# Top-32 attention feeding an expert layer: the eight fillers written by GpSimd in one operation, the weights' high halves rounded on ScalarE, and the order laid out anew

## The chip, the cores and the metric

The kernel runs on one core of a Trainium2 chip. The metric is the device time of one execution in microseconds (us). Engines are called as the profile calls them: PE is TensorE (PEld its weight loads), DVE is VectorE, ACT is ScalarE, POOL is GpSimd, SP is the queue that issues the DMAs.

## The reference, cut to what matters

```python
scores = scale * np.matmul(q, k.transpose(0, 1, 3, 2))      # 8 batches x 8 heads, 576 x 576, depth 64
kth = np.partition(scores, -32, axis=-1)[..., -32:-31]       # the 32nd largest of a row
mask = scores >= kth
scores = np.where(mask, scores, -1000000000.0)
attn = np.exp(scores - np.max(scores, axis=-1, keepdims=True))
attn = attn / (np.sum(attn, axis=-1, keepdims=True) + 1e-09)
x = np.matmul(attn, v)                                       # laid out as 4608 tokens x 512
...
r = np.maximum(x @ w_in, 0.0)                                # 512 -> 2048
out = (s * (r * r) + b) @ w_out                              # 2048 -> 512
```

The two weights arrive as 64-bit floats and are converted on the chip.

## The kernel before

**Tiles.** Attention runs over 288 tiles of 128 score rows by 576 columns. The expert layer runs over 18 blocks of 256 tokens, each in 16 chunks of 128 hidden units, so there are 288 chunks too. Products are taken with the operands split into a rounded high half and a remainder ("high" and "low"), which is why most operands exist twice (`ka`/`kb`, `ph`/`pl`, `gh`/`gl`, `wih`/`wil`, `woh`/`wol`). Batch 0 is kept whole, without low halves of the attention weights.

**One attention tile.** PE makes the scores in PSUM (L364), ACT copies them to `sc` (L370). DVE takes the eight largest of each of eight groups (L376) and works through the candidates with three more maxima and two replacements (L383 to L392); the last of them gives `wl`, whose column 15 is a cautious estimate of the 32nd largest. POOL makes a threshold from the high 16 bits of that estimate (`half`, L399) and the bias for the exponential (`max`, L404). ACT writes a sign for each score, minus above the threshold and plus below, and sums the signs into `cnt` (`side`, L411). POOL multiplies scores and signs into `wt` (`win`, L417). Behind the 576 signed scores stand 8 filler columns: some of them large and the rest very negative, so many of each, by the count, that the eighth largest of all 584 columns is just the 32nd largest score. DVE finds it (`wmax`, L435, into `chk`), then masks the exponentials that ACT made (`exp`, L429; `mask`, L439). PE transposes the masked tile into `tp` and `tq` (`put`, L468, L469), ACT and DVE split it (`high` L474, `low` L479), and PE multiplies with the values (L503 to L505).

**The fillers before.** They take three operations on two engines. `max` on POOL also zeroes the low 16 bits of `wl`'s column 15 (L405). `pad` on ACT writes eight signs from the count into a tile `pad` (L422), with two column operands (scale and bias). `fill` on ACT multiplies them with column 15 into the last eight columns of `wt` (L425), with one column operand; it waits for `win` and for `max`.

**The weights.** 64 pieces of 128 by 256 go through the chip: a load, three bit operations on DVE (`bits0` to `bits2`, L307 to L313), two squarings on ACT (`far0`, `far1`, L320 and L324) and a matmul (`far2`, L327) that guard the range, `whigh` on POOL (L330) that rounds the high half, and `wlow` on POOL (L333) that subtracts it. The pieces lie between the first tiles' work. The bank of PSUM in which `far2` adds up is the one that the hidden product `h` uses, so the expert layer starts when the last piece is through.

**One chunk of the expert layer.** PE makes `h` with 12 matmuls (L610), ACT applies relu and squares (L616, L619), POOL splits (`ghigh` L623, `glow` L627), PE adds 6 matmuls to the output (L633). At the end of a block DVE scales two results (L640) and SP stores them.

**What sets the order.** Every operation is entered into a list with its engine, a slot, a duration and an offset from the table `PARTS`. `Graph.order` plays the list through and gives each engine its fixed order; a tile's key is its number plus the offset, a chunk's key is `TURN0 + chunk / TURNS` plus the offset, a weight's key runs from 0 to `WTURN`. Among what could start within `SLACK` of the earliest, the smallest key goes first. Operations in `LOCK` (all of POOL's, DVE's `mask` and the bit operations) are kept from running on DVE and POOL at once in that play. On the chip each engine then runs its own order, and waits where an operand or a buffer isn't ready. There is one buffer each for `wt` and `sg`, two for `e`, four for `sc`.

## Time and profile before

| what | value |
|---|---|
| median of 3 runs | 1702.57 us (1700.66 to 1703.59) |
| the profiled execution | 1707.27 us, span 1705.5 us |
| before the expert layer starts | 0 to 305.6 us |
| attention and expert layer together | 305.6 to 1558 us |
| expert layer alone | 1558 to 1694 us |
| last store and the end | 1694 to 1705.5 us |

The span is the time from the first to the last instruction in the trace; the rest of the execution's time lies around it. The borders are read from the timeline: the first hidden matmul starts at 305.62 us, the last masked tile's work on DVE ends at about 1558 us, the last matmul of the expert layer ends at about 1694 us. A row of a group of instructions gives busy time, the mean duration in ns, the idle time of the engine just before, and what ended it. In a row of a tile the three durations are the least, the median and the largest. A row of waits gives the total in us, how many there were and the longest.

### The profile page before, as it was taken

To read this page: it belongs to the slowest core of one execution; us is meant where nothing else is said; L and a number is where in the kernel's file an instruction comes from. 1 tells how busy PE (TensorE), PEld (TensorE's weight loads), DVE (VectorE), ACT (ScalarE), POOL (GpSimd) and SP (SyncE) were. 2 spreads that over 40 slices of the span, in tenths; PEclk is the share of its full clock that TensorE was granted. 3 is DMA by queue.
4 is the path that set the end of the run, shared out by engine and by line. 5 is a ranking of instruction groups with operands and counts; after the bars stand their busy time and mean duration, and the time that the engine had idled before them with its cause. 6 is when DMAs were issued, how large, how long until landed. Compare 5 with 4: busy or idle time off the path is not lost. (4 is left out here: it accounts for less than half of the span.)

```text
span 1705.5 us, 34540 instructions
## 1 busy us (share of the span) xinstructions
PE 1494.9 (88%) x9361; PEld 1286.2 (75%) x9361; DVE 1404.7 (82%) x6055; ACT 1362.5 (80%) x3354; POOL 1233.6 (72%) x2176
## 2 busy tenths in 40 slices
...
GB/s 137 88 88 107 107 90 106 49 58 80 59 62 57 70 70 68 58 82 58 82 54 86 57 70 61 60 71 60 69 68 65 65 110 88 138 109 63 26 13 15
DMA packets 102123, 124.51 MB, mean 73 GB/s; under 512 B 30240, under 2 KB 65056, under 8 KB 101920
## 3 DMA queue, kind: packets, MB, share of 16 engines
...
q14 instruction: 126, 1.03, 0.2%
...
## 5 line engine op out<-in xcount | busy, mean ns | idle before, releaser
L417 POOL TENSOR_TENSOR wt<-sc,sg 128x576 f32<-128x576 f32 x288 | 399.7, 1388 | 95.7 <-ACT sg L411 40.3
L610 PE MATMUL h<-x,wih 128*128 128x256 f32 x2176 | 421.5, 288 | 17.4 <-ACT rt L616 16.4
L376 DVE MAX8 cand<-sc 128x8 f32<-128x72 f32 x2304 | 397.4, 219 | 34.6 <-ACT sc L370 32.1
L610 PEld LDWEIGHTS h<-x,wih 128*128 128x128 f32 x2176 | 347.6, 190 | 42.3 <-ACT rt L616 28.1
L610 PE MATMUL h<-x,wil 128*128 128x256 f32 x1088 | 307.3, 282 | 0.0
L439 DVE SCALAR_TENSOR_TENSOR e<-sc,chk,e 128x576 f32<-128x576 f32 x288 | 289.2, 1006 | 0.8
L435 DVE MAX8 chk<-wt 128x8 f32<-128x584 f32 x288 | 219.3, 761 | 50.2 <-ACT wt L425 40.9
L468 PE MATMUL tp<-idr,e 128*128 128x128 f32 x1152 | 191.2, 291 | 67.3 <-DVE e L439 38.0
L411 ACT ACTIVATE sg<-sc,nb 128x576 bf16<-128x576 int16 x288 | 221.7, 770 | 21.5 <-POOL nb L399 15.9
L370 ACT ACTIVATE sc<-s_ps 128x576 f32<-128x576 f32 x288 | 186.3, 647 | 64.8 <-DVE e L439 39.0
L627 POOL TENSOR_TENSOR gl<-rt,gh 128x256 fp32r<-128x256 f32 x288 | 220.8, 768 | 14.4 <-PE ops L633 3.8
L429 ACT ACTIVATE e<-sc,nb 128x576 f32<-128x576 f32 x288 | 221.9, 771 | 2.7 <-PE tq L469 2.5
L468 PEld LDWEIGHTS tp<-idr,e 128*128 128x128 f32 x1152 | 136.1, 147 | 115.0 <-DVE pl L479 38.8
L623 POOL TENSOR_SCALAR gh<-rt 128x256 fp32r<-128x256 f32 x288 | 127.5, 444 | 115.3 <-ACT rt L619 71.9
L610 PEld LDWEIGHTS h<-x,wil 128*128 128x128 f32 x1088 | 207.0, 190 | 0.0
L633 PE MATMUL ops<-woh,gh 128*128 128x512 f32 x576 | 192.8, 404 | 6.6 <-DVE osb L640 4.3
L474 ACT ACTIVATE ph<-tp 128x512 fp32r<-128x512 f32 (+1 forms) x288 | 171.1, 594 | 29.3 <-PE tp L468 26.2
L479 DVE TENSOR_TENSOR pl<-tp,ph 128x512 fp32r<-128x512 f32 x252 | 171.7, 681 | 26.5 <-ACT ph L474 23.5
L364 PE MATMUL s_ps<-ka,qs 128*128 128x288 f32 x512 | 164.5, 334 | 32.8 <-ACT sc L370 15.1
L633 PE MATMUL ops<-woh,gl 128*128 128x512 f32 x576 | 190.2, 402 | 0.4 <-POOL gl L627 0.4
L616 ACT ACTIVATE rt<-h 128x256 f32<-128x256 f32 x288 | 108.5, 377 | 101.7 <-PE h L610 96.5
L633 PE MATMUL ops<-wol,gh 128*128 128x512 f32 x576 | 188.0, 398 | 0.0
(101 smaller groups left out, 3502.1 us busy)
## 6 DMA issues: line engine op xcount, KB each, us to landing
...
qs<-ka SPq DMA_DIRECT2D x128, 64.0 KB, 2.0
qs<-kb SPq DMA_DIRECT2D x128, 64.0 KB, 2.0
```

The lines of the kernel that those rows point to most:

```text
L370: nc.scalar.activation(t.sc, t.flat, AF.Identity)
L376: nc.vector.max(t.cand[:, g * 8 : g * 8 + 8], t.sc[:, g * GW : (g + 1) * GW])
L411: nc.scalar.activation(t.sg, t.sc.bitcast(I16)[:, 1::2], AF.Sign, bias=t.half, scale=-1.0, accum_out=t.cnt[:, 0:1])
L417: nc.gpsimd.tensor_tensor(out=t.wt[:, :S], in0=t.sc, in1=t.sg, op=ALU.mult)
L429: nc.scalar.activation(t.e, t.sc, AF.Exp, bias=t.nb, scale=scale)
L435: nc.vector.max(t.pair.chk[:, t.i, 0:PADS], t.wt)
L439: nc.vector.scalar_tensor_tensor(t.e, t.sc, chk[:, PADS - 1 : PADS], t.e, op0=ALU.is_ge, op1=ALU.mult, accum_out=chk[:, PADS : PADS + 1])
L468: nc.tensor.transpose(tp[:, c, :], t.e[:, c * P : (c + 1) * P], idf)
L479: nc.vector.tensor_tensor(out=pl[:, :, dst], in0=t.tp, in1=ph[:, :, dst].bitcast(F32), op=ALU.subtract)
L610: nc.tensor.matmul(k.h, wi[a][:, cc, fs], k.x[cc][:, c, :], start=(cc == 0 and i == 0), stop=(cc == NCC - 1 and i == 2))
L627: nc.gpsimd.tensor_tensor(out=k.gl[fc], in0=k.rt[fc], in1=k.gh[fc].bitcast(F32), op=ALU.subtract)
L633: nc.tensor.matmul(k.ops[t], g[fc][:, t * P : (t + 1) * P], wo[w][:, fc, :], start=(fc == 0 and i == 0), stop=(fc == NFC - 1 and i == 2),)
```

## The change

The fillers become one operation on POOL, `pad`, ahead of `wmax`: it adds the count (a column) to a constant row and multiplies by -1e30, straight into the last eight columns of `wt`. The two operations on ACT, the memset in `max`, the tile `pad` and the column `one` go. `pad` needs `side` and `win`; `wmax` needs `pad`. The rounding of the weights' high halves goes from POOL to ACT, as an identity. The reduction of `chk` in `finish1` takes in one more column. The table's offsets, `SLACK` of POOL, `TURN0` and `WTURN` have other values, so each engine's order is another. The matmuls, the DMAs and the buffers other than `pad` are the same in number and size.

```diff
-    "whigh": ("POOL", 380, 430, 9.29), "wlow": ("POOL", 702, 740, -10.27), ...
+    "whigh": ("ACT", 306, 408, 9.29), "wlow": ("POOL", 702, 740, -6.52), ...
...
-    "half": ("POOL", 147, 190, -0.55), "max": ("POOL", 185, 230, -7.81), ...
+    "half": ("POOL", 147, 190, -0.68), "max": ("POOL", 125, 190, -7.26), ...
...
-    ... "pad": ("ACT", 70, 190, 1.55), "fill": ("ACT", 70, 190, -0.32), ...
+    ... "pad": ("POOL", 270, 310, -1.7), ...
...
-SLACK = {"PE": 0, "DVE": 86, "ACT": 0, "POOL": 67, "SP": 0}
-TURN0, TURNS = 48.1, 0.992
-WTURN = 34.2
+SLACK = {"PE": 0, "DVE": 86, "ACT": 0, "POOL": 0, "SP": 0}
+TURN0, TURNS = 49.4, 0.992
+WTURN = 40
...
-        nc.gpsimd.memset(pads[:, j : j + 1], -1.0 / (S - 2 * (TOPK - PADS + j) - 1))
-    one = const.tile([P, 1], F32, name="one")
-    nc.gpsimd.memset(one, 1.0)
+        nc.gpsimd.memset(pads[:, j : j + 1], float(2 * j - (S - 2 * (TOPK - PADS) - 1)))
...
         def high(w):
-            nc.gpsimd.tensor_scalar(w.dst[0][:, w.a, w.cs], w.lw.bitcast(F32), 1.0, 0.0, op0=ALU.mult, op1=ALU.add)
+            nc.scalar.activation(w.dst[0][:, w.a, w.cs], w.lw.bitcast(F32), AF.Identity)
...
         nc.gpsimd.tensor_scalar(t.nb, t.wl[:, 0:1], -scale, 0.0, op0=ALU.mult, op1=ALU.add)
-        nc.gpsimd.memset(t.wl.bitcast(I16)[:, 30:31], 0)
...
     def pad(t):
 
-        t.pad = sb.tile([P, PADS], F32, name="pad", tag="pad", bufs=BUFS["pad"])
-        nc.scalar.activation(t.pad, pads, AF.Sign, scale=t.cnt[:, 0:1], bias=one)
-
-    def fill(t):
-        nc.scalar.activation(t.wt[:, S:], t.pad, AF.Identity, scale=t.wl[:, 15:16])
+        nc.gpsimd.tensor_scalar(t.wt[:, S:], pads, t.cnt[:, 0:1], -PADK, op0=ALU.add, op1=ALU.mult)
...
-        nc.vector.tensor_reduce(tmin[:, 0, pr.i : pr.i + 1], pr.chk[:, :n, PADS - 1], axis=AX.X, op=ALU.min)
+        nc.vector.tensor_reduce(tmin[:, 0, pr.i : pr.i + 1], pr.chk[:, :n, PADS - 1 :], axis=AX.XY, op=ALU.min)
...
-            pb = Buf("pad")
-            pd = part("pad", i, lambda t=t: pad(t), [side_], [pb], [cnt])
-            pd = part("fill", i, lambda t=t: fill(t), [pd, win, mx], use=[pb, wt, wl])
+            pd = part("pad", i, lambda t=t: pad(t), [side_, win], use=[wt, cnt])
```

What the new order moves is shown at three places. The line numbers of the changed kernel are a few lower than those of the kernel before for the same operation.

The first is PE where the expert layer starts: `tp` and `tq` are a tile's transposes, `h` with `gh` the last pieces of the weights' guard, `h` with `x` the first hidden product. Before:

```order
L505 MATMUL av<-p_2974,vst 128x320
L327 MATMUL h<-gh,idr 128x256
L468 MATMUL tp<-idr,e 128x128 x4
L469 MATMUL tq<-idr,e 64x128
L610 MATMUL h<-x,wih 128x256 x2
L610 MATMUL h<-x,wil 128x256
L610 MATMUL h<-x,wih 128x256 x2
L610 MATMUL h<-x,wil 128x256
L364 MATMUL s_ps<-ka,qs 128x288
```

The same place in the changed kernel:

```order
L315 MATMUL ops<-x,bmat 128x256
L462 MATMUL tp<-idr,e 128x128 x4
L463 MATMUL tq<-idr,e 64x128
L326 MATMUL h<-gh,idr 128x256
L363 MATMUL s_ps<-ka,qs 128x288
L363 MATMUL s_ps<-kb,qs 128x288
L363 MATMUL s_ps<-ka,qs 128x288
L363 MATMUL s_ps<-kb,qs 128x288
L604 MATMUL h<-x,wih 128x256 x2
L604 MATMUL h<-x,wil 128x256
```

Counted from the start of PE's order, 44 tiles' transposes stand ahead of the first hidden matmul before, and 50 in the changed kernel. Ahead of the last tile's transposes stand 244.75 of the 288 chunks' hidden matmuls before, and 247 in the changed kernel.

The second is POOL in the stage in which both layers run: `wt` from `sc` and `sg` is `win`, `nb` from `wl` are `half` and `max`, `gh` and `gl` belong to the expert layer, `avu` is the sum of two halves of a result. Before:

```order
L417 TENSOR_TENSOR wt<-sc,sg 128x576
L623 TENSOR_SCALAR gh<-rt 128x256
L627 TENSOR_TENSOR gl<-rt,gh 128x256
L417 TENSOR_TENSOR wt<-sc,sg 128x576
L399 TENSOR_SCALAR nb<-wl 128x1
L404 TENSOR_SCALAR nb<-wl 128x1
L405 MEMSET wl 128x1
L530 TENSOR_TENSOR avu<-avu,avl 128x576
```

The changed kernel, with `wt` from `pads` and `cnt` the new `pad`:

```order
L415 TENSOR_TENSOR wt<-sc,sg 128x576
L398 TENSOR_SCALAR nb<-wl 128x1
L419 TENSOR_SCALAR wt<-pads,cnt 128x8
L403 TENSOR_SCALAR nb<-wl 128x1
L699 TENSOR_TENSOR kb<-kr,ka 128x576
L617 TENSOR_SCALAR gh<-rt 128x256
L415 TENSOR_TENSOR wt<-sc,sg 128x576
L621 TENSOR_TENSOR gl<-rt,gh 128x256
L419 TENSOR_SCALAR wt<-pads,cnt 128x8
```

The memset is gone and `pad` stands behind `win`, here with a `half` and then with a `gl` between them. Over all 288 tiles `pad` follows `win` at once in 73; a `half` or a `max` of another tile stands between them in 97, and a longer operation (a split, a sum, a spread) in most of the others.

The third is ACT in the stage with the weights: `x` from `x` is `far0`, `gh` is `far1`, `sg` is `side`. Before:

```order
L411 ACTIVATE sg,cnt<-sc,nb 128x576
L422 ACTIVATE pad<-pads,one,cnt 128x8
L513 ACTIVATE avu<-av 64x320
L320 ACTIVATE x<-x 128x256
L324 ACTIVATE gh<-x,mid 128x256
L320 ACTIVATE x<-x 128x256
L324 ACTIVATE gh<-x,mid 128x256
L370 ACTIVATE sc<-s_ps 128x576
```

The changed kernel:

```order
L409 ACTIVATE sg,cnt<-sc,nb 128x576
L507 ACTIVATE avu<-av 64x320
L319 ACTIVATE x<-x 128x256
L329 ACTIVATE wih<-x 128x256
L323 ACTIVATE gh<-x,mid 128x256
L409 ACTIVATE sg,cnt<-sc,nb 128x576
L369 ACTIVATE sc<-s_ps 128x576
```

`pad` and `fill` are gone from ACT's order, and a third operation for each piece of the weights stands there, between the two squarings.

More of the change, by code (lines that the diff above doesn't have):

```diff
@@ L27 @@
 PADS = 8
+PADK = 1.0e30
 NG = 8
@@ L41 @@
 PARTS = {
-    "wload": ("SP", 100, 3500, -1.07), "bits0": ("DVE", 195, 275, -6.39), "bits1": ("DVE", 330, 412, 5.98), "bits2": ("DVE", 325, 405, -2.85),
-    "colsum": ("PE", 470, 700, -7.2), "far0": ("ACT", 333, 438, -4.44), "far1": ("ACT", 414, 514, -1.14), "far2": ("PE", 119, 300, -8.25),
-    "whigh": ("POOL", 380, 430, 9.29), "wlow": ("POOL", 702, 740, -10.27), "farmax": ("DVE", 330, 420, -3.38), "bias": ("ACT", 264, 384, -1.61),
-    "kqload": ("SP", 100, 4500, 1.84), "kqhigh": ("ACT", 574, 678, -6.51), "kqlow": ("POOL", 1380, 1425, -4.35),
@@ L50 @@
-    "half": ("POOL", 147, 190, -0.55), "max": ("POOL", 185, 230, -7.81), "side": ("ACT", 759, 860, 0.26), "win": ("POOL", 1250, 1290, 1.48),
-    "exp": ("ACT", 666, 767, 7.53), "wmax": ("DVE", 668, 754, 0.3), "pad": ("ACT", 70, 190, 1.55), "fill": ("ACT", 70, 190, -0.32), "mask": ("DVE", 742, 825, -2.56),
-    "put": ("PE", 502, 690, -1.98), "high": ("ACT", 478, 595, 1.14), "low": ("DVE", 590, 675, -2.32),
-    "resth": ("ACT", 290, 392, 3.31), "restl": ("DVE", 520, 560, 5.2), "av": ("PE", 147, 330, 0.73), "avout": ("ACT", 320, 400, -9.13),
@@ new lines @@
+    "colsum": ("PE", 470, 700, -7.2), "far0": ("ACT", 333, 438, -3.63), "far1": ("ACT", 414, 514, -0.23), "far2": ("PE", 119, 300, -8.25),
+    "whigh": ("ACT", 306, 408, 9.29), "wlow": ("POOL", 702, 740, -6.52), "farmax": ("DVE", 330, 420, 0.61), "bias": ("ACT", 264, 384, -0.37),
+    "kqload": ("SP", 100, 4500, 0.64), "kqhigh": ("ACT", 574, 678, -6.51), "kqlow": ("POOL", 1380, 1425, -4.35),
+    "kplace": ("SP", 130, 3200, 5.84), "qplace": ("SP", 130, 3200, -3.31), "mplace": ("SP", 130, 3200, -4.93),
@@ new lines @@
+    "vload": ("SP", 100, 4500, 0.11), "vhigh": ("ACT", 360, 466, -0.75), "vlow": ("POOL", 830, 870, -1.1), "vkeep": ("SP", 100, 2500, 7.57),
+    "qk": ("PE", 132, 300, -3.91), "sc": ("ACT", 531, 648, -5.69), "group": ("DVE", 134, 218, 18.68),
+    "c0": ("DVE", 95, 173, 7.12), "c1": ("DVE", 157, 235, 4.84), "c2": ("DVE", 101, 188, -0.18), "c3": ("DVE", 161, 248, -0.57), "c4": ("DVE", 126, 208, -3.24),
+    "half": ("POOL", 147, 190, -0.68), "max": ("POOL", 125, 190, -7.26), "side": ("ACT", 759, 860, 0.26), "win": ("POOL", 1250, 1290, 2.58),
@@ new lines @@
+    "exp": ("ACT", 666, 767, 7.54), "wmax": ("DVE", 668, 754, 0.39), "pad": ("POOL", 270, 310, -1.7), "mask": ("DVE", 742, 825, -2.56),
+    "put": ("PE", 502, 690, -6.96), "high": ("ACT", 478, 595, 5.05), "low": ("DVE", 590, 675, -2.32),
+    "resth": ("ACT", 290, 392, 4.04), "restl": ("DVE", 520, 560, 12.35), "av": ("PE", 147, 330, 0.51), "avout": ("ACT", 320, 400, -9.2),
+    "sums": ("DVE", 340, 430, -1.68), "add": ("POOL", 1375, 1420, 3.82), "spread": ("POOL", 738, 780, 3.12), "turn": ("PE", 600, 800, -0.28),
@@ L59 @@
+    "scale": ("DVE", 900, 1000, -4.67), "xkeep": ("SP", 100, 2300, 10.1),
+    "xload": ("SP", 130, 3500, -11.58), "xhigh": ("ACT", 306, 405, -5.72), "xlow": ("POOL", 692, 735, -5.04),
+    "h": ("PE", 357, 540, 0.76), "relu": ("ACT", 263, 378, 7.88), "square": ("ACT", 306, 415, -2.73), "ghigh": ("POOL", 369, 405, 6.21),
+    "glow": ("POOL", 705, 745, 1.85), "o": ("PE", 231, 395, 3.13), "osb": ("DVE", 658, 742, 3.11), "store": ("SP", 100, 2400, 1.32),
 }
 LOCK = {"mask", "bits0", "bits1", "bits2", *(x for x, y in PARTS.items() if y[0] == "POOL")}
-SLACK = {"PE": 0, "DVE": 86, "ACT": 0, "POOL": 67, "SP": 0}
@@ L65 @@
-TURN0, TURNS = 48.1, 0.992
-WTURN = 34.2
+SLACK = {"PE": 0, "DVE": 86, "ACT": 0, "POOL": 0, "SP": 0}
+TURN0, TURNS = 49.4, 0.992
+WTURN = 40
 LATE = (16,)
-BUFS = dict(ph=1, pl=1, p4=1, avu=2, avl=1, x=4, osb=1, sc=4, wt=1, e=2, kr=1, sg=1, rt=2, gh=2, gl=2, vst=2, ka=2, kb=2, qs=2, s_ps=1, tp=1, tq=1, av=1, h=1, ops=2, cand=2, wl=3, m2=2, cnt=3, nb=2, chk=2, pad=2, ri=2)
+BUFS = dict(ph=1, pl=1, p4=1, avu=2, avl=1, x=4, osb=1, sc=4, wt=1, e=2, kr=1, sg=1, rt=2, gh=2, gl=2, vst=2, ka=2, kb=2, qs=2, s_ps=1, tp=1, tq=1, av=1, h=1, ops=2, cand=2, wl=3, m2=2, cnt=3, nb=2, chk=2, ri=2)
```

10 lines of the change are left out of this document (1 added, 9 removed).

## The prediction

> **What bounds the kernel now.** I read the page's first part, then the busy time of each engine in the stages, then who waits for whom in the stage that lasts longest, then single groups.
>
> ```profile
> span 1705.5 us, 34540 instructions
> PE 1494.9 (88%) x9361; PEld 1286.2 (75%) x9361; DVE 1404.7 (82%) x6055; ACT 1362.5 (80%) x3354; POOL 1233.6 (72%) x2176
> ```
>
> No engine is full over the span, so the stages have to be taken apart. In the table of stretches the columns are the five engines' busy time in the order of the first row.
>
> ```profile
> core 0: us, PE busy (x) PEld busy (x) DVE busy (x) ACT busy (x) POOL busy (x), PEclk, DMA share, GB/s
> 0.00:305.60 305.60, 201.29 (x767) 133.58 (x767) 257.62 (x1073) 220.41 (x513) 202.91 (x353) 0.79 0.37 103
> 305.60:1558.00 1252.40, 1157.75 (x7737) 1030.64 (x7736) 1136.07 (x4961) 1100.17 (x2736) 969.22 (x1719) 0.99 0.26 72
> 1558.00:1694.00 136.00, 135.04 (x856) 121.89 (x857) 8.82 (x18) 41.91 (x108) 61.49 (x106) 1.00 0.06 18
> ```
>
> The first stage (weights and the first tiles) is DVE's: 257.6 of 305.6 us. PE stands a third of it empty, with a granted clock of 0.79, since no chunk may start yet. The middle stage (244 tiles, 244.75 chunks by the order) has four engines close together: PE 92.4%, DVE 90.7%, ACT 87.8%, POOL 77.4%. The last stage is PE alone: a chunk there takes 1.44 + 1.39 = 2.83 us by the chain of waits.
>
> ```profile
> 1642.96 1.44 PE h L610 x12
> 1644.39 1.39 PE ops L633 x6
> ```
>
> So the middle stage decides. PE is idle in it for 1252.4 - 1157.75 = 94.65 us. Who made PE wait there:
>
> ```profile
> PE tp L468 <- DVE pl L479: 21.3, 39, 1.9
> PE tp L468 <- DVE e L439: 16.1, 25, 1.5
> PE h L610 <- ACT rt L616: 15.0, 23, 2.1
> PE s_ps L364 <- ACT sc L370: 10.8, 14, 2.4
> ```
>
> And whom DVE waited for there:
>
> ```profile
> DVE chk L435 <- ACT wt L425: 33.8, 39, 3.5
> DVE cand L376 <- ACT sc L370: 20.9, 12, 5.9
> DVE pl L479 <- ACT ph L474: 18.3, 27, 2.8
> ```
>
> PE waits for DVE (37.4 us in two rows) and for ACT (25.8 us in two rows), and DVE waits for ACT (73.0 us in three). The largest of these is the very operation that goes, `fill`. That is the case for the change.
>
> **The change part by part: ACT.** The groups over the whole run that the change touches:
>
> ```profile
> L422 ACT ACTIVATE pad<-pads,one,cnt 128x8 f32<-128x8 f32 x288 | 111.4, 387 | 1.2
> L425 ACT ACTIVATE wt<-pad,wl 128x8 f32<-128x8 f32 x288 | 84.5, 293 | 0.4
> L599 ACT ACTIVATE x<-x 128x256 fp32r<-128x256 f32 x68 | 25.1, 411 | 6.4 <-DMA x<-xd 6.2
> L330 POOL TENSOR_SCALAR woh<-x 128x256 fp32r<-128x256 f32 x32 | 18.3, 571 | 19.0 <-DVE x L313 18.9
> L330 POOL TENSOR_SCALAR wih<-x 128x256 fp32r<-128x256 f32 x32 | 16.3, 511 | 34.2 <-DVE x L313 34.2
> L399 POOL TENSOR_SCALAR nb<-wl 128x1 f32<-128x1 int16 x288 | 76.3, 265 | 113.4 <-DVE wl L392 102.3 <-PE ops L633 2.1 <-PE s_ps L551 1.9
> L405 POOL MEMSET wl<- 128x1 int16 x288 | 29.2, 101 | 0.0
> L521 DVE TENSOR_REDUCE tmin<-chk 128x1 f32<-128x9 f32 x28 | 4.2, 152 | 0.0
> ```
>
> ACT loses 387 + 293 = 680 ns for each tile, 288 x 0.680 = 195.9 us in all, and gains 64 roundings. One of 256 columns takes 411 ns there (the row of `x`), so 64 x 0.411 = 26.3 us. This is too kind to the change, because an ACT instruction starts before the one ahead has ended:
>
> ```profile
> 705.56 0.19 ACT L411 ACTIVATION_READ_ACCUMULATOR sg<-sc,nb 128x1 f32 x1
> 705.65 0.46 ACT L742 ACTIVATE vst<-kr 128x320 fp32r<-128x320 f32 x1
> ```
>
> Here the overlap is 0.10 us. With 0.10 us off each, the two operations occupy 480 ns, and the middle stage's 238 tiles lose 238 x 0.480 = 114 us of ACT rather than 238 x 0.680 = 162 us. I take 114: ACT would fall from 87.8% to (1100 - 114) / 1247 = 79% of the new middle stage worked out below, and a little lower with six tiles fewer. The Trainium skill, "ScalarE: Activation LUTs", section "What ACT_TABLE_LOAD costs", gives 186 ns + 0.833 ns a column, some 93 ns for each column operand, and an overlap of 93 ns back to back. By it `pad` would take 379 ns and `fill` 286 ns, 479 ns together without the overlaps; the two durations and the overlap seen here agree with it, and it speaks against booking the whole 196 us.
>
> **POOL.** It loses the memset (101 ns a tile, 29.2 us) and 34.6 us of roundings, all of the latter in the first stage. It gains 288 times `pad`, which the trace doesn't show. From below the nearest row is 192 ns, the median of a one-column operation, from above 408 ns, that of one of 256 columns:
>
> ```profile
> L399 POOL TENSOR_SCALAR nb<-wl x288: 182/192/837, 29.0 to 1551.8; 128x1 f32<-128x1 int16 x144
> L623 POOL TENSOR_SCALAR gh<-rt x241: 397/408/1016, 314.5 to 1552.0; 128x256 fp32r<-128x256 f32 x121
> ```
>
> Eight columns are near the small end, and the column operand costs something on top (on ACT two against one made 387 - 293 = 94 ns). I take 265 ns, the mean of L399 with its waits: 238 x (0.265 - 0.101) = 39 us more of POOL in the middle stage, 0.16 us a tile. At below nothing, that is as a gain, it could end too: with `fill` gone `wmax` no longer stands behind ACT's queue, which cost 33.8 us above. But in 215 of 288 places another operation of POOL stands between `win` and `pad`, so that part of this wait comes back with POOL's name. `pad` itself waits for nothing that `win` hasn't waited for. Behind `wmax` in DVE's queue stand the next tile's maxima and the tile's own `mask`, and behind `mask` PE's transposes, whose 16.1 us row is quoted above.
>
> **The rounding moved.** On POOL it waited for DVE's bits, 34.2 + 18.9 us in the two L330 rows; on ACT it stands behind `far0`, which waits for the same bits, and so adds no new wait there. What is queued behind it on ACT is 0.41 us later each time, 26 us against the 50 x 0.48 = 24 us that the fillers free in this stage. I book nothing; DVE, which bounds the stage, covers it. If that cover were gone it would cost up to 2 us. The loads keep their number, and on SP they are spread over six tiles more. DVE waited for them mostly at the start:
>
> ```profile
> DVE rt L307 <- DMA x<-in_moe_w_in_dram: 13.2, 8, 4.4
> ```
>
> By PE's order 8 and 9 pieces are through ahead of the first transposes, so I leave these 13.2 us as they are; later loads have more time than before. The wider reduction in `finish1` comes 32 times. Twice its columns cost at most twice its row, some 4 us over the run, and it stands at the end of a pair of heads, where DVE turns to the next pair's maxima; I book nothing, and 4 us if that cover is gone.
>
> **The order.** This is the largest term. Six more tiles pass DVE before the first chunk (50 against 44). A tile costs DVE (1136.07 - 21.5) / 244 = 4.57 us in the middle stage, without the output scaling:
>
> ```profile
> L640 DVE SCALAR_TENSOR_TENSOR osb<-ops,s_col,bias 128x512 f32<-128x512 f32 x29 | 21.5, 742 | 7.9 <-DMA out_dram<-osb 4.5 <-PE ops L633 3.1
> ```
>
> So the first stage grows by 6 x 4.57 = 27.4 us. Against it stand DVE's waits for ACT in this stage:
>
> ```profile
> DVE cand L376 <- ACT sc L370: 11.2, 15, 2.7
> DVE chk L435 <- ACT wt L425: 6.8, 9, 2.5
> ```
>
> That is 18.0 us, of which I let a quarter go, 4.5 us, since ACT's load stays as it was here: first stage +23 us.
>
> The middle stage then has 238 tiles and 247 chunks. A tile costs PE (1157.75 - 244.75 x 2.83) / 244 = 1.91 us. PE's work is 1157.75 - 6 x 1.91 + 2.25 x 2.83 = 1152.7 us. At the same share of 92.4% that takes 1247 us: -5.4 us. The last stage has 2.25 chunks fewer: -6.4 us. The sum at an unchanged share of PE is 23 - 5.4 - 6.4 = +11.2 us. The profiled execution would go from 1707.27 to 1718.5 us. The median of the runs lies 4.7 us below that execution, so I set the same difference on it: 1702.57 + 11.2 = 1713.8, rounded to **1714 us**.
>
> I take the share as unchanged because two loads move against each other. ACT falls by some 9 points or more. DVE and POOL share the work that cannot run together: `mask` took 810 ns in the median and 2048 at most, with a mean of 1006 ns over the run, when POOL was in its way.
>
> ```profile
> L439 DVE SCALAR_TENSOR_TENSOR e<-sc,chk,e x242: 792/810/2048, 310.7 to 1556.3; 128x576 f32<-128x576 f32 x121
> L439 DVE SCALAR_TENSOR_TENSOR e<-sc,chk,e 128x576 f32<-128x576 f32 x288 | 289.2, 1006 | 0.8
> ```
>
> POOL's 969.2 us and 242 x 0.81 = 196 us of masks are 1165 of 1252 us, 93%, as full as PE. A tile costs POOL (969.2 - 241 x (0.444 + 0.768)) / 244 = 2.8 us without the expert layer's splits:
>
> ```profile
> L623 POOL TENSOR_SCALAR gh<-rt 128x256 fp32r<-128x256 f32 x288 | 127.5, 444 | 115.3 <-ACT rt L619 71.9
> L627 POOL TENSOR_TENSOR gl<-rt,gh 128x256 fp32r<-128x256 f32 x288 | 220.8, 768 | 14.4 <-PE ops L633 3.8
> ```
>
> With `pad` and six tiles fewer the pair becomes 969 + 39 - 17 + 238 x 0.81 = 1184 of 1247 us, 95%.
>
> **The rivals.** *ACT's relief carries through (faster).* If the waits named above that ACT causes, and PE's for a late DVE, shrink by a little under half, some 30 of PE's 94.65 us of idle go: 1152.7 + 64.6 = 1217 us, -35 us. With +23 and -6.4 that is -18.4 us, **1684 us**. It decides from 11.2 us of idle removed, a share of 93.3%. For it speaks the 33.8 us row; against it, that ACT's relief is smaller than its durations, and that DVE's load per us stays. Chance 0.33.
>
> *The pair POOL and `mask` becomes the bound (slower still).* `pad` adds 238 x 0.265 = 63 us to what `mask` can't run beside. If a third of it shows, 21 us, the sum is +32 us, **1735 us**; it decides where `pad` starts late enough for `wmax` to wait. By the Trainium skill, "SBUF — State Buffer", section "Who interferes with whom", a DVE instruction with two SBUF inputs and a GpSimd one that reads SBUF exclude each other for the whole instruction, while one that only writes doesn't; the stretched masks agree with the first half, and by the second the memset that goes freed nothing. Chance 0.17.
>
> *It comes out even.* Some 8 to 15 us of PE's idle go and pay for the longer first stage. Chance 0.12.
>
> **How the numbers follow.** The forecast (1706 to 1725 us) has 0.38. Slower by over 0.2% (3.4 us, about what a measurement of this kernel can tell from no change) is 0.38 + 0.17 = 0.55, the same 0.12, faster 0.33. The slower cases alone span 1706 to 1740. The range goes from 1684, which leaves out half of the first rival, to 1736, which leaves out a small part of the second: some 0.2 in all.
>
> **What would show it.** Right: the first hidden matmul at 323 to 333 us; PE's share between there and the last masked tile at 92 to 93%; the last stage near 130 us; ACT at 76 to 79% in the middle; `pad` at 0.2 to 0.3 us; a row "chk waits for POOL wt" of 15 to 35 us in place of L425. Wrong: a share of PE above 93.3%, or a first stage below 318 us, either of which would make it faster than said; masks with a mean above 1100 ns would point to the pair of POOL and DVE.

## The result, and the profile after

The changed kernel takes 1674.41 us (median of 4 runs, 1673.78 to 1675.24) beside 1702.22 us for the kernel before (4 runs, 1700.66 to 1703.59): a ratio of 0.9837 (95% interval 0.982 to 0.9854), 1.6% faster. The forecast was 1714 us with a range from 1684 to 1736: the time moved the other way and lies 9.6 us below that range. The profiled execution of the changed kernel took 1674.74 us, that of before 1707.27 us. The spans differ by 32.5 us, the medians by 27.8 us, because before's profiled execution lay 5.1 us above its median and the new one 0.3 us.

The first part of the changed kernel's page has the span, and each engine's busy time over it:

```profile
span 1673.0 us, 33649 instructions
PE 1486.4 (89%) x9361; PEld 1285.3 (77%) x9361; DVE 1393.2 (83%) x6055; ACT 1251.0 (75%) x2842; POOL 1292.3 (77%) x2111
```

ACT lost 111 us and POOL gained 59. That says nothing yet of where 32.5 us went; the stages do. The prediction put the border between the middle and the last stage of before at 1558 us, where DVE's last mask ends. PE's last transposes come 7.5 us later, and since PE is the engine that is counted, I use them for all kernels from here on. These are the middle and the last stage of before with that border (columns: stretch, its length, then busy time of PE, PEld, DVE, ACT and POOL, the granted clock, DMA share and GB/s):

```profile
305.60:1565.50 1259.90, 1164.89 (x7787) 1037.27 (x7787) 1140.35 (x4971) 1104.06 (x2746) 975.92 (x1729) 0.99 0.26 72
1565.50:1694.50 129.00, 128.35 (x809) 115.29 (x807) 4.77 (x8) 38.03 (x96) 54.79 (x96) 1.00 0.04 14
```

And the three stages of the changed kernel in the same columns:

```profile
0.00:320.30 320.30, 211.85 (x853) 141.72 (x854) 273.57 (x1196) 233.55 (x527) 195.42 (x315) 0.82 0.35 102
320.30:1539.30 1219.00, 1152.22 (x7742) 1033.76 (x7741) 1112.92 (x4847) 980.97 (x2224) 1043.61 (x1705) 1.00 0.26 73
1539.30:1662.00 122.70, 122.07 (x770) 109.73 (x768) 4.74 (x8) 36.48 (x93) 53.23 (x93) 1.00 0.04 15
```

The first stage is 14.7 us longer, the last 6.3 us shorter, and the middle 40.9 us shorter. In the middle, PE's idle time went from 1259.9 - 1164.9 = 95.0 us to 1219.0 - 1152.2 = 66.8 us, and its busy time fell by 12.7 us. PE's share rose from 92.5% to 94.5%. Cut into twelve equal slices, the middle has idle PE time in every slice, 5.4 to 12.1 us before and 3.0 to 10.8 us after: no single event was removed. The granted clock explains little of it. By the trace's clock records 8.5 us of the middle were lost to a lower clock before, and 5.1 us in the changed kernel.

Whom PE waited for in the middle of the changed kernel (us in total, times, longest):

```profile
PE tp L462 <- DVE e L433: 12.5, 24, 1.5
PE tp L462 <- DVE pl L473: 10.4, 19, 1.4
PE s_ps L363 <- ACT sc L369: 9.4, 13, 2.7
PE h L604 <- ACT rt L610: 8.0, 16, 1.2
```

The prediction took the rows of before up to 1558 us. Up to the border used here three of them are larger, and a row that it did not show, `p`, is added:

```profile
PE h L610 <- ACT rt L616: 16.1, 24, 2.1
DVE chk L435 <- ACT wt L425: 34.1, 40, 3.5
DVE pl L479 <- ACT ph L474: 20.5, 28, 2.8
DVE p L489 <- ACT p L484: 0.6, 2, 0.4
```

All four of PE's rows have shrunk, `pl` (21.3 to 10.4 us) and `rt` (16.1 to 8.0 us) by half. Whom DVE waited for in the middle of the changed kernel:

```profile
DVE cand L375 <- ACT sc L369: 33.2, 34, 4.1
DVE pl L473 <- ACT ph L468: 23.2, 21, 4.9
DVE chk L429 <- POOL wt L419: 7.6, 20, 1.6
DVE p L483 <- ACT p L478: 7.0, 9, 1.9
```

The wait for the fillers, 34.1 us before, is 7.6 us under POOL's name. But the others grew: `cand` went from 20.9 to 33.2 us, `ph` from 20.5 to 23.2 us, `p` from 0.6 to 7.0 us. These rows of DVE sum to 71.0 us instead of 76.1, PE's four to 40.3 instead of 64.3: most of the vanished wait came back under other names on DVE, and PE still gained.

The groups that the change touched, and the masks, over the whole run (busy us, mean ns of one, idle before):

```profile
L419 POOL TENSOR_SCALAR wt<-pads,cnt 128x8 f32<-128x8 f32 x288 | 112.0, 389 | 27.3
L433 DVE SCALAR_TENSOR_TENSOR e<-sc,chk,e 128x576 f32<-128x576 f32 x288 | 281.5, 979 | 1.7
L306 DVE TENSOR_SCALAR rt<-x 128x256 int32<-128x256 int32 x64 | 23.8, 372 | 18.5 <-DMA x<-in_moe_w_in_dram 15.7 <-DMA x<-in_moe_w_out_dram 2.4
L329 ACT ACTIVATE woh<-x 128x256 fp32r<-128x256 f32 x32 | 13.5, 424 | 0.0
```

And the durations of the new `pad` on POOL (least, median, largest):

```profile
L419 POOL TENSOR_SCALAR wt<-pads,cnt x288: 270/271/982, 35.9 to 1534.9; 128x8 f32<-128x8 f32 x144
```

### The profile page after: what moved, and what is told of

Read it like the earlier page. It is cut to its first block, busy times and chain, and to the rows that moved or that the text cites. A ratio compares the mean times of both kernels' runs of the same rounds, so it can differ in the third digit from the quotient of the medians.

```text
span 1673.0 us, 33649 instructions
## 1 busy us (share of the span) xinstructions
PE 1486.4 (89%) x9361; PEld 1285.3 (77%) x9361; DVE 1393.2 (83%) x6055; ACT 1251.0 (75%) x2842; POOL 1292.3 (77%) x2111
## 4 chain that ended last, share of the span: by engine, by line
PE 37%; DVE 33%; ACT 9%; DMA 6%; POOL 5%; issue 5%; SPq 4%; POOLq 0%; ACTq 0%; DVEq 0%
PE h L604 12%; PE ops L627 11%; DVE cand L375 8%; DVE e L433 6%; DVE chk L429 4%; DVE pl L473 4%; PE tp L462 4%; PE s_ps L363 4%; SPq L709 2%; DMA kr<-in_kq_dram 2%; ACT sc L369 2%; ACT sg L409 2%; PE av L493 1%; DVE cand L384 1%; POOL wt L415 1%
## 5 line engine op out<-in xcount | busy, mean ns | idle before, releaser
L375 DVE MAX8 cand<-sc 128x8 f32<-128x72 f32 x2304 | 392.2, 219 | 44.5 <-ACT sc L369 43.4
L433 DVE SCALAR_TENSOR_TENSOR e<-sc,chk,e 128x576 f32<-128x576 f32 x288 | 281.5, 979 | 1.7
L462 PE MATMUL tp<-idr,e 128*128 128x128 f32 x1152 | 188.4, 288 | 64.3 <-DVE e L433 35.1
L621 POOL TENSOR_TENSOR gl<-rt,gh 128x256 fp32r<-128x256 f32 x288 | 217.3, 757 | 12.2 <-PE ops L627 1.3
L610 ACT ACTIVATE rt<-h 128x256 f32<-128x256 f32 x288 | 109.1, 379 | 122.7 <-PE h L604 112.9
L617 POOL TENSOR_SCALAR gh<-rt 128x256 fp32r<-128x256 f32 x288 | 123.2, 430 | 79.1 <-PE ops L627 57.1
```

Of the source, the lines that this page charges most:

```text
L375: nc.vector.max(t.cand[:, g * 8 : g * 8 + 8], t.sc[:, g * GW : (g + 1) * GW])
L433: nc.vector.scalar_tensor_tensor(t.e, t.sc, chk[:, PADS - 1 : PADS], t.e, op0=ALU.is_ge, op1=ALU.mult, accum_out=chk[:, PADS : PADS + 1])
L462: nc.tensor.transpose(tp[:, c, :], t.e[:, c * P : (c + 1) * P], idf)
```

## The experiments

In the table "ahead" is the number of tiles' transposes in PE's order ahead of the first hidden matmul, the stages end at the first hidden matmul, the last transposes and the last output matmul, and "idle" is PE's in the middle. Stage times come from one profiled execution of each kernel, which lay up to 5.5 us from the median of that kernel's runs, so differences of a few us between stages say little. The time of the kernel before, measured beside each of them on the same chip, lay between 1703.8 and 1705.4 us.

| kernel | median us | ratio to before (95%) | ahead | first | middle | idle | last |
|---|---|---|---|---|---|---|---|
| before | 1702.2 | 1 | 44 | 305.6 | 1259.9 | 95.0 | 129.0 |
| after | 1674.4 | 0.9837 (0.982 to 0.9854) | 50 | 320.3 | 1219.0 | 66.8 | 122.7 |
| e1_newwork_oldnumbers | 1696.0 | 0.9943 (0.9918 to 0.9967) | 44 | 296.4 | 1253.1 | 82.8 | 128.3 |
| e2_oldwork_newnumbers | 1707.9 | 1.0026 (1.0004 to 1.0048) | 50 | 333.1 | 1240.7 | 82.7 | 126.7 |
| e3_fillers_only | 1707.7 | 1.0013 (0.9996 to 1.003) | 50 | 340.5 | 1230.0 | 71.5 | 123.0 |
| e4_rounding_only | 1703.9 | 0.9993 (0.9976 to 1.0011) | 49 | 313.7 | 1246.7 | 85.9 | 126.8 |
| e5_scalar_load_back | 1712.0 | 1.0057 (1.0034 to 1.008) | 50 | 324.0 | 1249.2 | 87.0 | 123.1 |
| e6_gpsimd_load | 1703.4 | 1.0001 (0.9984 to 1.0018) | 50 | 319.5 | 1248.2 | 85.2 | 122.9 |
| e7_rounding_writes_only | 1706.6 | 1.003 (1.0012 to 1.0047) | 50 | 340.9 | 1229.4 | 71.2 | 123.1 |
| e8_early_start | 1698.3 | 0.9975 (0.9956 to 0.9993) | 44 | 302.8 | 1255.4 | 84.1 | 128.3 |
| e9_rounding_gpsimd_same_order | 1674.9 | 0.9824 (0.9791 to 0.9856) | 50 | 319.6 | 1215.3 | 67.3 | 122.7 |
| e10_rounding_scalar_other_order | 1709.2 | 1.0026 (1.0008 to 1.0044) | 50 | 340.6 | 1230.4 | 68.9 | 123.0 |
| e11_turn0_only | 1689.4 | 0.9891 (0.9855 to 0.9928) | 50 | 321.2 | 1230.6 | 75.1 | 125.1 |
| e12_wturn_only | 1706.4 | 1.0006 (0.9986 to 1.0026) | 44 | 302.8 | 1261.1 | 87.2 | 124.4 |
| e13_oldwork_wturn_only | 1701.4 | 0.9981 (0.9965 to 0.9997) | 49 | 324.3 | 1233.2 | 79.1 | 128.2 |
| e14_oldwork_turn0_only | 1711.3 | 1.0035 (1.002 to 1.0051) | 44 | 305.8 | 1268.7 | 96.4 | 126.9 |
| e15_newwork_shift1 | 1737.9 | 1.0204 (1.0168 to 1.0241) | 50 | 328.7 | 1259.9 | 97.4 | 134.0 |
| e16_oldwork_shift1 | 1714.7 | 1.0068 (1.0044 to 1.0092) | 44 | 304.3 | 1267.0 | 96.4 | 126.9 |
| e17_newwork_shift2 | 1701.4 | 0.9984 (0.9973 to 0.9996) | 50 | 329.6 | 1232.3 | 67.9 | 123.0 |
| e18_oldwork_shift2 | 1715.0 | 1.0066 (1.0049 to 1.0083) | 44 | 300.7 | 1271.0 | 96.2 | 128.3 |

### The work or the numbers?

Two theories stood at the start: ACT's relief carries through (the prediction's first rival), or the new numbers, and so the new order, give the gain. `e1_newwork_oldnumbers` has the new operations with before's offsets (`pad`, now another operation, keeps its own), SLACK, TURN0 and WTURN:

```diff
-SLACK = {"PE": 0, "DVE": 86, "ACT": 0, "POOL": 0, "SP": 0}
+SLACK = {"PE": 0, "DVE": 86, "ACT": 0, "POOL": 67, "SP": 0}
-TURN0, TURNS = 49.4, 0.992
+TURN0, TURNS = 48.1, 0.992
-WTURN = 40
+WTURN = 34.2
```

> The changed kernel's work (fillers on GpSimd, rounding on ScalarE) with the numbers of before (offsets, SLACK, TURN0, WTURN). 44 tiles ahead of the first chunk, as before. If ScalarE's relief makes the gain: the middle stage loses some 25 to 30 us of PE's idle as in the changed kernel, and the first stage is as short as before (306 us), so 1665 to 1685 us. If the numbers make it: near 1702 us or above, 1695 to 1715.

`e2_oldwork_newnumbers` is the reverse, before's operations with the changed kernel's numbers (the same lines with the signs turned, and the offsets).

> The work of before with the changed kernel's numbers. 50 tiles ahead of the first chunk. If ScalarE's relief makes the gain: PE's idle in the middle stays near 95 us and the first stage is 15 us longer, 1705 to 1720 us. If the numbers make it: 1670 to 1685 us.

The middle of each, with the columns as above; first `e1_newwork_oldnumbers`:

```profile
296.40:1549.50 1253.10, 1170.33 (x7789) 1040.91 (x7787) 1144.13 (x4972) 998.67 (x2258) 1059.65 (x1726) 0.99 0.26 72
```

then `e2_oldwork_newnumbers`:

```profile
333.10:1573.80 1240.70, 1158.03 (x7715) 1027.52 (x7714) 1128.88 (x4845) 1083.91 (x2692) 962.20 (x1701) 1.00 0.26 72
```

The work alone gives a third of the gain (0.9943), the numbers alone none (1.0026). In the middle each takes 12 us from PE's idle time (95.0 to 82.8 and 82.7), and both together 28. The numbers pay for theirs with a first stage 27.5 us longer. So neither theory's expectations hold: the work alone loses less idle time than ACT's relief was to bring, the numbers alone bring no time at all, and the gain comes from the two together.

### Which part of the work?

`e3_fillers_only` takes the rounding back to POOL and leaves the rest of the changed kernel:

```diff
-    "whigh": ("ACT", 306, 408, 9.29), ...
+    "whigh": ("POOL", 380, 430, 9.29), ...
...
-            nc.scalar.activation(w.dst[0][:, w.a, w.cs], w.lw.bitcast(F32), AF.Identity)
+            nc.gpsimd.tensor_scalar(w.dst[0][:, w.a, w.cs], w.lw.bitcast(F32), 1.0, 0.0, op0=ALU.mult, op1=ALU.add)
```

> The changed kernel with the rounding of the weights' high halves left on GpSimd. If the fillers alone make the gain: within 5 us of the changed kernel, 1670 to 1680 us, with a first stage within 5 us of its 320 us. If the rounding matters: 1685 us or more.

`e4_rounding_only` is before with the new numbers and only the rounding moved to ACT (the two lines above, turned, in `before`).

> The changed kernel's numbers and its rounding on ScalarE, with the fillers as before (two operations on ScalarE and the memset). If the fillers make the gain: PE's idle in the middle near 95 us, 1705 to 1725 us. If the rounding makes it: 1675 to 1690 us.

Neither alone is measurably faster. The first and middle stages of `e3_fillers_only`:

```profile
0.00:340.50 340.50, 222.27 (x852) 149.14 (x853) 292.87 (x1205) 223.98 (x469) 237.37 (x385) 0.77 0.35 97
340.50:1570.50 1230.00, 1158.55 (x7740) 1037.26 (x7739) 1118.72 (x4838) 978.69 (x2217) 1042.59 (x1697) 0.99 0.26 72
```

With the fillers and the new numbers most of the idle time in the middle is gone (71.5 us left), but the first stage is 340.5 us against 320.3. DVE is busy 292.9 us in it instead of 273.6, and POOL 237.4 instead of 195.4. The next runs ask two things: does ACT's load count in the middle, and what makes this first stage 20 us longer?

### Load put back into the same order

`e5_scalar_load_back` gives ACT the two small operations back, into tiles that nobody reads, with every engine's order otherwise as in the changed kernel. So ACT has its old load, and DVE does not wait for it:

```diff
@@ side
+        j1 = sb.tile([P, PADS], F32, name="ja", tag="ja", bufs=1)
+        nc.scalar.activation(j1, pads, AF.Sign, scale=s_col, bias=b_col)
@@ expo
+        j2 = sb.tile([P, PADS], F32, name="jb", tag="jb", bufs=1)
+        nc.scalar.activation(j2, pads, AF.Identity, scale=s_col)
```

> The changed kernel with every engine's order unchanged, but for two operations of 128x8 in each tile on ScalarE that write a scratch tile which nobody reads (one with two column operands behind the signs, one with one behind the exponentials): ScalarE's load of the old fillers without VectorE's wait for them. If ScalarE's load is what the middle stage gained from: PE's idle there rises from 67 us by 10 to 20 us, 1685 to 1700 us. If it is that the maximum no longer waits behind ScalarE's queue: within 5 us of the changed kernel, 1672 to 1680 us.

`e6_gpsimd_load` doubles `pad` on POOL, again into a tile that nobody reads:

```diff
@@ pad
+        jp = sb.tile([P, PADS], F32, name="jp", tag="jp", bufs=2)
+        nc.gpsimd.tensor_scalar(jp, pads, t.cnt[:, 0:1], -PADK, op0=ALU.add, op1=ALU.mult)
```

> The changed kernel with the filler operation issued a second time right behind itself, into a scratch tile that nobody reads, all else in the same order. If the pair of GpSimd and the mask is near its bound: 63 us of its time are added in the middle and a third or more shows, 1690 us or more. If GpSimd has room: 1673 to 1682 us.

The middle of `e5_scalar_load_back`:

```profile
324.00:1573.20 1249.20, 1162.21 (x7743) 1032.01 (x7742) 1118.87 (x4847) 1083.25 (x2698) 1040.42 (x1705) 0.99 0.26 72
```

its two added groups on ACT:

```profile
L414 ACT ACTIVATE ja<-pads,b_col,s_col 128x8 f32<-128x8 f32 x288 | 109.9, 382 | 0.0
L428 ACT ACTIVATE jb<-pads,s_col 128x8 f32<-128x8 f32 x288 | 84.4, 293 | 0.0
```

and whom PE waited for in its middle:

```profile
PE tp L467 <- DVE pl L478: 15.0, 29, 1.4
PE tp L467 <- DVE e L438: 14.9, 28, 1.5
PE h L609 <- ACT rt L615: 14.8, 25, 2.0
PE s_ps L363 <- ACT sc L369: 14.4, 20, 2.3
```

The load alone, without the wait for the fillers, takes the whole gain away, more than either expectation said: 1712.0 us, a middle 30.2 us longer, PE idle 20.2 us more. ACT's own rows (`rt`, `sc`) rise from 17.4 to 29.2 us. ACT, 80% busy, was thus not free to take its old load back. The middle of `e6_gpsimd_load`:

```profile
319.50:1567.70 1248.20, 1162.99 (x7743) 1032.14 (x7742) 1124.21 (x4847) 982.17 (x2225) 1115.53 (x1941) 1.00 0.26 72
```

72 us more on POOL make the middle 29.2 us longer. So it is not ACT that is special: in this order 0.30 us of time come with each us of busy time added to ACT (30.2 / 102.3), and 0.41 us with each added to POOL (29.2 / 71.9). These are prices of adding to an order that was made without the load, and they do not carry over to the change itself. `e2` and the changed kernel have the same numbers and 50 tiles ahead, and differ in the work: the new work takes 102.9 us off ACT's busy time in the middle and adds 81.4 us to POOL's. By these prices that is worth 30 - 33 us, about nothing, but the middle is 21.7 us shorter. From before to `e1` it is 105.4 us off and 83.7 us on, again about nothing by the prices, and the middle is 6.8 us shorter. So `e5` and `e6` show that this order has room for neither load. They don't show how much of the gain is ACT's relief, how much the vanished wait, and how much the fit of the order to the durations.

### The rounding and the longer first stage

My first reading of `e3_fillers_only` was that POOL's rounding reads SBUF and so stands in DVE's way: its masks in the first stage took 1092 ns in the mean, against 938 in the changed kernel. The row of these masks in `e3_fillers_only`:

```profile
L478 DVE SCALAR_TENSOR_TENSOR e<-sc,chk,e 128x576 f32<-128x576 f32 x51 | 55.5, 1092 | 0.1
```

and in the changed kernel:

```profile
L433 DVE SCALAR_TENSOR_TENSOR e<-sc,chk,e 128x576 f32<-128x576 f32 x50 | 46.8, 938 | 0.7
```

`e7_rounding_writes_only` is `e3_fillers_only` in the same order with an operation that only writes. It leaves the rounding out: the high halves are a constant.

```diff
-            nc.gpsimd.tensor_scalar(w.dst[0][:, w.a, w.cs], w.lw.bitcast(F32), 1.0, 0.0, op0=ALU.mult, op1=ALU.add)
+            nc.gpsimd.memset(w.dst[0].bitcast(F32)[:, w.a, w.cs], 0.5)
```

> As the run with the fillers alone (rounding left on GpSimd, same order on every engine), but the rounding is a memset of the same 128x256: it writes and doesn't read, so the high halves are a constant and the remainder is not the weights' own. If the first stage is long (340 us) because GpSimd's reading operation and VectorE's two-input operations exclude each other: the first stage falls to 320 to 330 us. If it is long because the remainder waits for GpSimd's own queue: it stays at 335 to 342 us.

Its first stage and its two groups of the new operation:

```profile
0.00:340.90 340.90, 224.17 (x852) 150.51 (x853) 293.51 (x1206) 223.60 (x469) 220.88 (x385) 0.77 0.35 97
```

```profile
L374 POOL MEMSET woh<- 128x256 f32 x32 | 10.0, 313 | 0.6
L374 POOL MEMSET wih<- 128x256 f32 x32 | 9.9, 311 | 0.5
```

The masks stayed long as well:

```profile
L478 DVE SCALAR_TENSOR_TENSOR e<-sc,chk,e 128x576 f32<-128x576 f32 x51 | 53.5, 1052 | 0.1
```

POOL has 16 us less to do in the stage, the replaced operation no longer reads, and the stage is as long as in `e3` (340.9 against 340.5 us). That explanation fell. By the Trainium skill, "SBUF — State Buffer", section "Who interferes with whom", a GpSimd operation that only writes does not exclude a DVE operation with two inputs in SBUF; this run neither confirms nor contradicts it, since POOL's other operations still read. It shows only that the rounding's reads are not where these 20 us come from.

What was left was the order. `e9_rounding_gpsimd_same_order` rounds on POOL, but is planned as if on ACT, so that everything else stands as in the changed kernel; `e10_rounding_scalar_other_order` rounds on ACT in the order of `e3_fillers_only`:

```diff
@@ e9: table as after, high() on POOL
-            nc.scalar.activation(w.dst[0][:, w.a, w.cs], w.lw.bitcast(F32), AF.Identity)
+            nc.gpsimd.tensor_scalar(w.dst[0][:, w.a, w.cs], w.lw.bitcast(F32), 1.0, 0.0, op0=ALU.mult, op1=ALU.add)
@@ e10: high() as after, table planned for POOL
-    "whigh": ("ACT", 306, 408, 9.29), ...
+    "whigh": ("POOL", 380, 430, 9.29), ...
```

> The changed kernel with the 64 roundings issued on GpSimd, at the places in time where they stood on ScalarE; every other instruction of every engine in the changed kernel's order. If the roundings' time on GpSimd is what makes the first stage long: it goes from 320 to 335 us or more, 1688 to 1700 us. If it is the order that the plan makes for them there: the first stage stays at 320 to 325 us, 1673 to 1680 us.

> The order that was planned with the roundings on GpSimd (the run with the fillers alone), but the roundings issued on ScalarE at those places. If the roundings' time on GpSimd makes the first stage long: it falls from 340 to 320 to 326 us, 1684 to 1692 us. If the planned order does: it stays at 335 us or more, 1700 to 1708 us.

The first two stages of `e9_rounding_gpsimd_same_order`:

```profile
0.00:319.60 319.60, 210.20 (x853) 140.10 (x854) 279.08 (x1196) 220.64 (x465) 230.72 (x379) 0.83 0.36 102
319.60:1534.90 1215.30, 1148.01 (x7741) 1029.53 (x7741) 1113.63 (x4848) 980.95 (x2223) 1044.19 (x1705) 1.00 0.26 73
```

its roundings on POOL:

```profile
L329 POOL TENSOR_SCALAR wih<-x 128x256 fp32r<-128x256 f32 x32 | 18.6, 581 | 16.0 <-DVE x L312 15.7
L329 POOL TENSOR_SCALAR woh<-x 128x256 fp32r<-128x256 f32 x32 | 16.9, 531 | 10.9 <-DVE x L312 10.6
```

and the first stage of `e10_rounding_scalar_other_order`:

```profile
0.00:340.60 340.60, 220.93 (x853) 146.22 (x854) 287.72 (x1205) 242.05 (x533) 201.48 (x321) 0.79 0.34 97
```

POOL does 35 us more in the first stage of `e9`, and the time is that of the changed kernel (1674.9 us). ACT does the rounding in `e10`, and the time is that of `e3` (1709.2 against 1707.7 us). The masks of its first stage take 1042 ns in the mean, close to `e3` and `e7`, so they go with the order too. Nor can the remainder's wait in POOL's queue behind the rounding be the reason, since the rounding isn't in that queue in `e10`. Where the rounding runs is worth under 2 us here; the order that the planner makes when it is told so is worth 34 us, 21 of them in the first stage. The runs also show how well a stage's time repeats: `e3`, `e7` and `e10`, three kernels in one order, have middles of 1230.0, 1229.4 and 1230.4 us.

### The later start

The changed kernel starts the expert layer later. `e8_early_start` is the changed kernel with before's TURN0 and WTURN; `e11_turn0_only` takes TURN0 alone back, `e12_wturn_only` WTURN alone. `e13_oldwork_wturn_only` and `e14_oldwork_turn0_only` are before with one of the new values:

```diff
@@ e8 (both lines), e11 (the first pair), e12 (the second pair), on after
-TURN0, TURNS = 49.4, 0.992
+TURN0, TURNS = 48.1, 0.992
-WTURN = 40
+WTURN = 34.2
@@ e13, on before
-WTURN = 34.2
+WTURN = 40
@@ e14, on before
-TURN0, TURNS = 48.1, 0.992
+TURN0, TURNS = 49.4, 0.992
```

> The changed kernel with TURN0 and WTURN of before: 44 tiles ahead of the first chunk instead of 50, all offsets new. If the later start of the expert layer is what makes the middle dense: PE's idle there rises to 80 us or more and the time to 1685 us or more. If it is the offsets: idle stays near 67 us, the first stage falls to about 296 us, and the time to 1660 to 1672 us.

> The changed kernel with TURN0 of before (48.1) and its own WTURN: still 50 tiles ahead of the first chunk, 246 chunks ahead of the last tile. If the chunks' place against the tiles (TURN0) makes the middle dense: PE's idle there rises to 80 us or more, 1685 to 1700 us. If not: idle 63 to 72 us, 1670 to 1680 us.

> The changed kernel with WTURN of before (34.2) and its own TURN0: 44 tiles ahead of the first chunk. If the early end of the weights makes the middle loose: PE's idle 80 us or more, first stage about 302 us, 1690 to 1700 us. If not: idle 63 to 72 us with the short first stage, 1660 to 1672 us, which would beat both kernels.

> The kernel before with WTURN 40: 49 tiles ahead of the first chunk. If a late start makes the middle dense whatever the work is: PE's idle there falls from 95 us to 80 us or less, 1685 to 1700 us. If it only fits the new work's numbers: idle 83 us or more, 1702 to 1720 us.

> The kernel before with TURN0 49.4: still 44 tiles ahead of the first chunk. If the numbers before were fitted to the old work as the new ones are to the new: 1710 to 1730 us. If the old work has no such peak: 1700 to 1708 us.

WTURN sets the start: with 40, `e11` has 50 tiles ahead and `e13` 49; with 34.2, `e12` has 44, whatever TURN0 says. The old work with WTURN 40 alone (`e13`):

```profile
324.30:1557.50 1233.20, 1154.14 (x7721) 1029.48 (x7720) 1121.25 (x4861) 1079.57 (x2699) 967.52 (x1703) 0.99 0.27 73
```

PE's idle time there is 79.1 us against 95.0, with ACT as full as before. So a later start makes the middle denser without the new work too, and the longer first stage (324.3 us) takes it back: 1701.4 us, above the 1685 to 1700 that were expected. `e8` says the same from the other side: the new work with an early start keeps 84.1 us of idle time and takes 1698.3 us. With WTURN alone taken back (`e12`) it is 87.2 us of idle time and 1706.4 us, slower than the expected 1690 to 1700. TURN0 alone moves the time as well: by 0.5% in the new work (`e11`, idle time 75.1 us, between its two expectations) and by 0.35% in the old (`e14`). Both kernels thus have a TURN0 that suits their own order.

### How much of it is the particular order?

Small random shifts of all offsets (up to half a tile's number) make a neighbouring order of the same work. Two sets of shifts were tried on both kernels, `e15` and `e17` on after, `e16` and `e18` on before. Of the first set on after:

```diff
-    "max": ("POOL", 125, 190, -7.26), ... "win": ("POOL", 1250, 1290, 2.58),
+    "max": ("POOL", 125, 190, -7.53), ... "win": ("POOL", 1250, 1290, 2.67),
-    "exp": ("ACT", 666, 767, 7.54), ... "mask": ("DVE", 742, 825, -2.56),
+    "exp": ("ACT", 666, 767, 7.04), ... "mask": ("DVE", 742, 825, -2.83),
...
```

> The changed kernel with every offset shifted by a random number within half a tile (first set). If the new work itself gains: 1680 to 1697 us, below the kernel before. If the fitted numbers are all of it: 1700 us or more.

> The kernel before with the same random shifts (first set). If the new work itself gains: 1705 to 1725 us, at least 10 us above the changed kernel with these shifts. If the fitted numbers are all of the gain: within 6 us of it.

> The changed kernel with every offset shifted by a random number within half a tile (second set). If the new work itself gains: 1680 to 1697 us. If the fitted numbers are all of it: 1700 us or more.

> The kernel before with the same random shifts (second set). If the new work itself gains: 1705 to 1725 us, at least 10 us above the changed kernel with these shifts. If the fitted numbers are all of the gain: within 6 us of it.

The old work moves by 0.7% with either set. The new work goes from 0.9837 to 1.0204 with the first and 0.9984 with the second. Side by side, the new work is 23.2 us slower than the old under the first set and 13.6 us faster under the second. The expectations set the new work's own gain against a gain that is all in the fitted numbers, and the two sets answer differently. The middle of `e15_newwork_shift1`:

```profile
328.70:1588.60 1259.90, 1162.48 (x7673) 1033.44 (x7672) 1135.94 (x4845) 985.93 (x2213) 1042.88 (x1696) 0.99 0.26 71
```

and the two rows that lead among PE's waits in it:

```profile
PE tp L507 <- DVE e L478: 24.1, 38, 1.2
PE tp L507 <- DVE pl L518: 13.7, 25, 1.1
```

PE waits twice as long for masks as in the changed kernel (24.1 us against 12.5), though DVE, ACT and POOL are busy within 2.1% of the same time. Its last stage is longer too, 134.0 against 122.7 us, since only 242.5 chunks stand ahead of its last tile's transposes instead of 247. Why this order lets masks come late was not settled.

Taken together, PE's idle time in the middle falls into four groups. Old work, early start (before, `e14`, `e16`, `e18`): 95.0 to 96.4 us. Old work, late start (`e2`, `e13`, and `e4`, which has the old fillers): 79.1 to 85.9. New work, early start (`e1`, `e8`, `e12`): 82.8 to 87.2. New work, late start (after, `e3`, `e11`, `e17`, with `e7`, `e9` and `e10`, which have the order of `e3` or after): 66.8 to 75.1, with one exception, `e15` at 97.4. Against before, each of the two effects alone takes 8 to 16 us off, and apart from `e15` they add up.

The idle time is not the whole of it. `e17` has 67.9 us of it, about as little as the changed kernel, and takes 1701.4 us: its first stage is 9.3 us longer, and PE's busy time in its middle 12.2 us. `e3`, `e7` and `e10` lose their gain mostly in a first stage of some 340 us. Of the late starts of the new work without added load, only the changed kernel, `e9` and `e11` keep the first stage below 322 us, and these are the three fastest of all.

## Why the prediction was wrong

**The step that failed** is "At the same share of 92.4% that takes 1247 us", in the part on the order. PE's share did not stay: it rose to 94.5%. The span was to grow by 11.2 us and shrank by 32.5. Of these 43.7 us, 35.5 lie in the middle (40.9 us shorter where 5.4 were booked), and 28.2 of its 40.9 us are PE's idle time. The reason given for an unchanged share was that "two loads move against each other". That weighed stage averages, and two things were missing in it. First, the two loads did not cancel: with the start kept early, the new work took 8 to 12 us off PE's idle time (`e1`, `e8` and `e12` against before). Loads put back into the changed kernel's order bring idle time back, 20.2 us for ACT's (`e5`, with the wait behind ACT's queue still gone) and 18.4 us for POOL's (`e6`), so the loads count also without the named wait; how the new work's gain divides between them stays open. Second, the later start was booked only as a cost of the first stage; it makes the middle denser too, also with the old work (`e2`, `e4`, `e13`). Why it does is open: no run separates the spread of the weights over more tiles from the six tiles of lead that the attention then has.

**The first rival** had the right size: 30 us of PE's idle time gone, where 28.2 went, and a share above 93.3%, the prediction's own sign of being wrong. Its reason, ACT's relief, is at most one part: the new work alone takes 12.2 of these 28.2 us (`e1`), and the later start with the old work 12.3 to 15.9 us (`e2`, `e13`). It gave 1684 us; the step from there to 1674 is a first stage 8.3 us shorter than booked and 7.6 us less of PE's busy time, against 1.8 us less of idle time saved and the 4.7 us by which the medians differ less than the spans.

**PE's work in the middle.** I booked 6 x 1.91 us less and 2.25 x 2.83 us more, together -5.1 us; PE's busy time fell by 12.7 us. The forecast of 1152.7 us met 1152.2 by luck: it took the chunks up to the last transposes (1565.5 us) but PE's busy time only up to 1558. With both up to 1565.5 us the same sum gives about 1160 us. Nor is PE's busy time a fixed quantity of work: in `e5` it is 1162.2 us for 7743 matmuls, in the changed kernel 1152.2 for 7742. Busy time counts a moment once however many matmuls run in it, and they overlap, as a row of the changed kernel shows (2176 x 288 ns are 627 us):

```profile
L604 PE MATMUL h<-x,wih 128*128 128x256 f32 x2176 | 421.6, 288 | 11.4 <-ACT rt L610 8.3 <-POOL x L597 1.9 <-ACT x L593 0.6
```

By the traces the matmuls' durations in the middle sum to 4 us more in `e5`, and overlap by 6 us less, with 178 breaks in PE's work instead of 151. That suggests that a wait costs PE some busy time too.

**The first stage** was booked at +23 us and was +14.7. The count of tiles is about right. These are the masks and the first bit operation of before in that stage:

```profile
L439 DVE SCALAR_TENSOR_TENSOR e<-sc,chk,e 128x576 f32<-128x576 f32 x45 | 43.7, 976 | 0.1
L307 DVE TENSOR_SCALAR rt<-x 128x256 int32<-128x256 int32 x64 | 29.8, 466 | 15.7 <-DMA x<-in_moe_w_in_dram 13.2 <-DMA x<-in_moe_w_out_dram 2.0
```

The masks went from 45 to 50. But DVE's busy time rose by 16.0 us where 27.4 was booked, since other work in the stage became cheaper: the bit operation fell from 29.8 to 23.8 us and a mask from 976 to 938 ns. Why is open. The spread of the weights over more tiles is not enough of a reason: `e3` has the same WTURN, and its bit operation takes 28.5 us. Of the 4.5 us of DVE's waits that I let go, 1.3 went (idle 48.0 us before, 46.7 after). And the term hangs on the order: with as many tiles ahead it is +35 us in `e3`.

**The last stage** was booked at -6.4 us and was -6.3. **The rounding**, booked at nothing, is worth nothing by itself (`e9`), with 424 ns each on ACT; but planning it on ACT gave the changed kernel the order with the short first stage (`e10`).

**Sizes on ACT and POOL.** ACT lost 114 us by the working; put back (`e5`), the two operations made 102.3 us of its busy time in the middle, 0.43 us a tile for 0.675 us of durations. By the Trainium skill, "ScalarE: Activation LUTs", section "What ACT_TABLE_LOAD costs", instructions back to back overlap by some 93 ns each; two overlaps leave 0.49 us a tile, so the trace agrees roughly and shows a little more. `pad` takes 271 ns in the median where 265 was taken, but 389 in the mean (383 in the middle). That is 237 x 0.118 = 28 us of the 46 by which POOL's busy time in the middle outgrew the working (+67.7 us, where 39 - 17 = 22 was booked); for most of the rest, the memset that went had lain beside other work of POOL, as the groups' durations there sum to only 49 us more. "chk waits for POOL wt" is 7.6 us in the middle, not 15 to 35, and the masks' mean is 979 ns, below the 1006 of before, so **the second rival** was not what happened. More load on POOL does cost time in this order: 72 us more cost 29 us (`e6`). Why `pad` did not show as a net loss no run separates; the same change freed ACT.

**What stays open.** Among its neighbours (`e1`, `e8`, `e11`, `e12`, `e15`, `e17`) the new work ranges from 0.9891 to 1.0204, with a mean of 1.000; the old work's (`e2`, `e13`, `e14`, `e16`, `e18`) from 0.9981 to 1.0068, with a mean of 1.0035. On the average of its neighbours the new work is only some 0.35% faster than the old. So the 1.6% belong to the pair of this work and this order; how often another order of the new work would reach it, eleven neighbours do not say. No version beat the changed kernel: `e9` equals it.
